# The first part of a scan-and-experts kernel in the order in which it is written, on every engine

## The chip, the cores and the metric

The kernel runs on one core of a Trainium2 chip. The metric is the time of one execution on the device, in microseconds (us); lower is better. The engines are TensorE (PE in the profile, its weight loads PEld), VectorE (DVE), ScalarE (ACT), GpSimd (POOL) and SyncE (SP), which here only issues transfers. A "q" behind an engine's name (SPq, POOLq) is its sequencer: branches, semaphores and the issuing of transfers.

## The reference

```python
def _attn_ref(x, f_logit, lower_bound):          # x, f_logit: (4, 5056, 256)
    sig = 1.0 / (1.0 + np.exp(-f_logit))
    f = lower_bound[None, None, :] + (1.0 - lower_bound[None, None, :]) * sig
    i = 1.0 - f
    for t in range(S):
        h = f[:, t] * h + i[:, t] * x[:, t]
        y[:, t] = h
...
def _moe_ref(x, w_gate, w_output_gate, w1, w2):  # 20224 tokens, 8 experts, 256 -> 1024 -> 256
    logits = x @ w_gate
    e_idx = np.argmax(logits, axis=1)
    ...                                          # gate_w: softmax probability of the chosen expert
    eom = 1.0 / (1.0 + np.exp(-(x @ w_output_gate)))
    for e in range(E):
        mask = e_idx == e
        h = np.maximum(x[mask] @ w1[e], 0.0)
        out[mask] = gate_w[mask, None] * eom[mask, e, None] * (h @ w2[e])
```

A gated running average over each sequence, and then every token through the one expert of eight that its gate picks.

## The kernel before

**Chunks.** The 20224 tokens are taken in 40 chunks of up to 512. `chunk(c)` is a generator: ACT and DVE scan the chunk, scale it and split it into two 16-bit halves; PE computes the gate (`pr`) and, from the one-hot choice `oh`, each token's rank in its expert (`pk`); DVE makes row numbers (`dst`) and factors (written into the rows' `meta`); SyncE transposes the halves into `rows`, and POOL scatters the rows by expert into a table in device memory (`scr`). Each bare `yield` ends a phase; `pump` runs one phase of every live chunk, with `together` mixing their small DVE instructions. Small tiles such as `dst` and `fac` come from pools with a fixed number of buffers (two where nothing else is said).

**Weights.** Ahead of the main part, 16 half-experts' weights are loaded, scaled and split into 16-bit parts: `prep_gram` (PE), `prep_norm`, `prep_scale` and `prep_lo` (DVE), `prep_hi` (ACT). The loop over `j` and its two half-steps `z` does this, and each half-step calls `step`, which pumps the chunks.

**First tiles.** In the same half-steps, 16 tiles of 128 tokens (two rounds over the experts) go through the experts that are ready. `early` gathers a tile (`gather`: a transposing transfer into `xq` and a small one into `mt`, both on SyncE's queue, after a load of the row number from a plan's table `pf_tab`), `first1` multiplies by w1 in two halves, `first_low` makes the low part of the result on DVE, `first2` multiplies by w2, `factors` makes the output factor `fac` from `mt`, `evacuate` scales (ACT), `put` scatters to the output (POOL).

**Main part.** `experts` runs 64 tiles of 256 tokens and 18 of 128 in the same manner, with the remaining chunks pumped between. Behind it stand 19 more tiles of 128 in two conditional blocks, run only if the plan counted more than 18 (`MORE`); with these inputs none runs.

**What sets the order.** A scheduler orders each engine's instructions by a simulated timeline, unless they are tied. `ordered` ties every instruction to the one written before it on its engine, except that ahead of `cut` (the end of the first part) it leaves DVE, ACT, PE and POOL loose:

```python
free = i < cut and ins.engine in loose
if ins.engine in prev and not free:
    tc.add_manual_dep(ins, prev[ins.engine], AFTER, reason="order")
```

So SyncE's queue is in the written order throughout, the others only from the main part on.

Of the kernel before, what the change touches and what calls it, by code (L numbers as in the profile page):

```python
# [50 lines left out]
def tile_scan_moe(  # L51
# [124 lines left out]

    gsq = cp.tile([P, KD * G], F32, name="gsq")
    gss = cp.tile([P, 1], BF16, name="gss")
# [31 lines left out]
    nc.gpsimd.iota(padt[:, CM + 2 : CM + 4].bitcast(I32), pattern=[[0, 1]], base=N, channel_multiplier=0)  # L210
    fresh.append(nc.sync.dma_start(out=scr[FREE : FREE + P, :], in_=padt))
    apart(fresh[0], "scr")
    row2 = [cp.tile([P, NB, RW], I16, name=f"rows{i}") for i in range(2)]
# [410 lines left out]
    def gather(t, slot, e=None):  # L624
        tab, j, nb, new = slot
        n = nb * P
        r = nc.sync.value_load(tab[j : j + 1, 0:1], min_val=0, max_val=FREE + P - n)
        xq = gp.tile([P, 2, KD, 256], I16, tag="xq", name="xq")
        mt = gp.tile([P, 2, 4], I16, tag="mt", name="mt", bufs=4)
        i1 = nc.sync.dma_start_transpose(  # L630
            out=xq.rearrange("p a k n -> p (a k) n")[:, :, 0:n], in_=scr[ds(r, n), 0 : 2 * D]
        )
        i2 = nc.sync.dma_start(out=mt[:, 0:nb, :], in_=scr[ds(r, n), CM : CM + 4].rearrange("(b p) d -> p b d", p=P))
        for ins in (i1, i2):
            for k in new:
                tc.add_manual_dep(raw(ins), raw(k).name, DATA, reason="rows scattered")
            apart(ins, "scr", new)
        return dict(xh=xq[:, 0].bitcast(F16), xl=xq[:, 1].bitcast(F16), mt=mt, nb=nb, tab=tab, j=j, id=t, ev=e)
# [5 lines left out]
    def factors(T):  # L644
        nb, ev = T["nb"], T["ev"]
        col = cinv[:, ev : ev + 1] if isinstance(ev, int) else cinv[:, ds(ev, 1)]
        fac = sp.tile([P, 2], F32, tag="fac", name="fac", bufs=4)
        yield SMALL
        nc.vector.tensor_scalar(  # L649
            fac[:, 0:nb].unsqueeze(2), T["mt"][:, 0:nb, 0:2].bitcast(F32), col, None, ALU.mult  # L650
        )
        T["fac"] = fac

# [68 lines left out]
    def first_low(T, h):  # L722
        ph, hh = T[f"h{h}"]
        hl = ep.tile([P, 4, P], F16, tag="el", name="el", bufs=3)
        yield BIG
        nc.vector.scalar_tensor_tensor(out=hl, in0=ph, scalar=0.0, in1=hh, op0=ALU.max, op1=ALU.subtract)
        T[f"h{h}"] = (hh, hl)
# [103 lines left out]
    def early(j):  # L831

        if not line or line[0]["half"] == 1 and len(line) == 1:
            for r in range(len(firsts)):
# [11 lines left out]
        for T, h in wait:  # L846
            tasks.append(first_low(T, h))
            if h == 0:
                tasks.append(factors(T))
# [27 lines left out]
    for n in range(min(EARLY[0], NCH) - 1, deep):  # L877
        prep_load(n)
    for j in range(-2, nh):
        tasks = []  # L880
# [29 lines left out]

    def ordered(start, cut):

        loose = [e.engine for e in (nc.vector, nc.scalar, nc.tensor, nc.gpsimd)]
        prev = {}
        for i, ins in enumerate(nc.cur_bb.bb.instructions[start:]):
            free = i < cut and ins.engine in loose
            if ins.engine in prev and not free:
                tc.add_manual_dep(ins, prev[ins.engine], AFTER, reason="order")
# [39 lines left out]
    between["on"] = True  # L958
    experts(0, total + cuts[0], len(cuts) - 1)
    beside()  # L960
    ordered(0, prog["cut"])

    if len(cuts) > 1:
        used = nc.values_load(prog["count"][0:1, 0:1], min_val=0, max_val=tail)  # L964
        for a, b in zip(cuts[:-1], cuts[1:]):
            with tc.If(used > a):
                experts(total + a, total + b, 0)
                ordered(0, 0)

# [37 lines left out]
```

## Time and profile before

| | us |
|---|---|
| median of three runs | 989.25 (988.75 to 989.73) |
| the profiled execution, its own time | 990.77 |
| its span, first to last instruction | 989.1 |
| busy in the span: PE, DVE, ACT, POOL | 907.7, 801.0, 519.7, 390.1 |
| the first matmul of the main part starts | 184.5 |
| the last output row is issued | 973.5 |
| mean granted PE clock | 0.988 |

Times in the rows are microseconds from the span's start. A row of a stretch gives its length, each engine's busy time with the count of instructions, the granted clock, the busy share of the 16 DMA engines and GB/s. A row of waits reads "who waited, for whom: us in all, times, longest". A row in order of time reads start, duration, engine, line, operation, tile written, tiles read, and in brackets the idle time ahead of it with what ended it. A row of one line's instructions gives shortest, median and longest duration in ns, and the first and last start.

### The profile page before, as it was taken

The page shows a single profiled execution, that of the slowest core. Times are in us where ns is not written, and L with a number is a line of the kernel's source. Part 1 is how long each engine was busy: PE and PEld are TensorE (multiplying, and loading weights), DVE is VectorE, ACT ScalarE, POOL GpSimd, SP SyncE. Part 2 cuts the span into 40 slices and gives each one's busy share as a digit, 9 for nine tenths or more (in the row PEclk, how much of TensorE's full clock was granted, in tenths as well). Part 3 has the DMA queues.
Part 4 walks back from the last instruction along what each step waited for, and adds up shares of the span by engine and source line. Part 5 has one row for each costly group of instructions (what it writes and reads, how often), then busy time and mean ns, then how long its engine had stood idle before and what let it go on. Part 6 is the DMA issues. An engine that isn't in the chain of part 4 may idle for free. (4 is left out here: it accounts for less than half of the span.)

```text
span 989.1 us, 30907 instructions
## 1 busy us (share of the span) xinstructions
PE 907.7 (92%) x9775; PEld 819.7 (83%) x9775; DVE 801.0 (81%) x2639; ACT 519.7 (53%) x1075; POOL 390.1 (39%) x378
## 2 busy tenths in 40 slices
PE   2258898899999999999999999999999999999993
PEld 2247887788888888888888888888888888899992
DVE  7989897888989988888898888888888886545550
ACT  6667675555555555555565555555555543333331
POOL 1432334434445454454545434455444443211111
PEclk9999999999999999999999999999999999999997
DMA  8899984855575657556576665655666544312120
GB/s 310 206 275 293 237 230 126 188 157 151 131 157 144 151 153 167 141 133 152 150 153 150 169 138 140 153 148 157 150 163 134 129 100 90 100 45 43 41 57 17
DMA packets 238558, 146.56 MB, mean 148 GB/s; under 512 B 202557, under 2 KB 204223, under 8 KB 238400
## 3 DMA queue, kind: packets, MB, share of 16 engines
q1 hardware_dynamic: 222752, 101.74, 44.9%
q0 software_dynamic: 15360, 42.74, 14.4%
q8 instruction: 95, 1.56, 0.7%
q14 instruction: 63, 0.52, 0.2%
q10 hardware_dynamic: 288, 0.02, 0.0%
HBM read 58.38 MB, written 44.49 MB: 104 GB/s over the span
## 5 line engine op out<-in xcount | busy, mean ns | idle before, releaser
L674 ACT ACTIVATE hh<-ph 128x512 f16<-128x512 f32 (+1 forms) x328 | 180.4, 550 | 307.8 <-PE ph L671 297.4
L669 PE MATMUL ph<-xq,w 128*128 128x256 f16 (+1 forms) x1312 | 330.4, 260 | 2.9 <-DMA xq<-scr 2.4
L671 PE MATMUL ph<-xq,w 128*128 128x256 f16 (+1 forms) x1312 | 331.1, 261 | 0.0
L670 PE MATMUL ph<-xq,w 128*128 128x256 f16 (+1 forms) x1312 | 330.9, 261 | 0.0
L750 POOL DMA_INDIRECT out_dram<-yo,mt x146 | 175.3, 1201 | 363.2 <-ACT yo L746 339.9
L704 PE MATMUL py<-w2s,hl 128*128 x1168 | 318.5, 273 | 0.0
L703 PE MATMUL py<-w2s,hh 128*128 x1168 | 318.4, 273 | 0.0
L702 PE MATMUL py<-w2s,hh 128*128 x1168 | 318.1, 272 | 0.0
L682 DVE SCALAR_TENSOR_TENSOR hl<-ph,hh 128x512 f16<-128x512 f32 (+1 forms) x328 | 204.9, 625 | 58.2 <-ACT hh L674 55.8
L433 POOL DMA_INDIRECT scr<-rows,dst x154 | 175.7, 1141 | 122.6 <-issue 109.3
L657 DVE COPY w<-w1s 128x2048 f16 x164 | 120.3, 734 | 35.1 <-PE ph L671 33.3
L669 PEld LDWEIGHTS <-w 128*128 128x128 f16 x1312 | 127.9, 98 | 14.3 <-DVE fac L649 2.7
L671 PEld LDWEIGHTS <-w 128*128 128x128 f16 x1312 | 128.0, 98 | 11.9
L670 PEld LDWEIGHTS <-w 128*128 128x128 f16 x1312 | 127.9, 97 | 9.7
L704 PEld LDWEIGHTS <-hl 128*128 128x128 f16 x1168 | 114.1, 98 | 13.8
L702 PEld LDWEIGHTS <-hh 128*128 128x128 f16 x1168 | 114.0, 98 | 11.4
L703 PEld LDWEIGHTS <-hh 128*128 128x128 f16 x1168 | 113.9, 98 | 10.6
L280 DVE TENSOR_TENSOR_SCAN xt<-ft,xt 128x512 f32<-128x512 f32 (+4 forms) x78 | 90.8, 1172 | 0.0
L746 ACT ACTIVATE yo<-py,fac 128x256 f32<-128x256 f32 x146 | 61.8, 468 | 26.7 <-PE py L704 26.1
L314 DVE SCALAR_TENSOR_TENSOR ft<-xt,sa,ft 128x512 f16<-128x512 f32 (+1 forms) x76 | 56.2, 744 | 20.1 <-ACT ft L265 18.3
L329 PEld LDWEIGHTS <-ft 128*128 128x128 f16 x600 | 51.7, 99 | 15.1 <-ACT ft L310 4.9
L310 ACT ACTIVATE ft<-xt,sa 128x512 f16<-128x512 f32 (+1 forms) x76 | 50.2, 707 | 23.3 <-DVE li L299 16.0
(171 smaller groups left out, 1298.7 us busy)
## 6 DMA issues: line engine op xcount, KB each, us to landing
ft<-in_fT_dram SPq DMA_DIRECT2D x37, 512.0 KB
xt<-in_xT_dram SPq DMA_DIRECT2D x37, 512.0 KB
w<-in_wT_dram SPq DMA_DIRECT2D x32, 512.0 KB
scr<-rows,dst POOLq DMA_INDIRECT x154
rows<-ft SPq DMA_TRANSPOSE x152
out_dram<-yo,mt POOLq DMA_INDIRECT x146
xq<-scr SPq DMA_TRANSPOSE x99
scr<-padt SPq DMA_DIRECT2D x9, 136.0 KB
```

What stands on the lines that cost most here:

```text
L280: nc.vector.tensor_tensor_scan(out=xt[:, k, a:z], data0=ft[:, k, a:z], data1=xt[:, k, a:z], initial=init, op0=ALU.mult, op1=ALU.add)
L433: ins = nc.gpsimd.indirect_dma_start(out=scr[:, :], out_offset=IOA(ap=dst[:, b : b + 1], axis=0), in_=rows[:, b, :], in_offset=None)
L657: nc.vector.tensor_copy(out=w, in_=w1f[:, ds(T["ev"] * (2 * WH) + h * 2 * QH, 2 * QH)])
L669: nc.tensor.matmul(out=o, lhsT=w[:, f, k, 0, :], rhs=T["xh"][:, k, 0:n], start=first, stop=False)
L670: nc.tensor.matmul(out=o, lhsT=w[:, f, k, 0, :], rhs=T["xl"][:, k, 0:n], start=False, stop=False)
L671: nc.tensor.matmul(out=o, lhsT=w[:, f, k, 1, :], rhs=T["xh"][:, k, 0:n], start=False, stop=last)
L674: nc.scalar.activation(hh[:, :, 0:n], ph[:, :, 0:n], AF.Relu)
L682: nc.vector.scalar_tensor_tensor(out=hl[:, :, 0:n], in0=ph[:, :, 0:n], scalar=0.0, in1=hh[:, :, 0:n], op0=ALU.max, op1=ALU.subtract)
L702: nc.tensor.matmul(out=o, lhsT=hh[:, i, c], rhs=wh, start=first, stop=False, skip_group_check=True)
L703: nc.tensor.matmul(out=o, lhsT=hh[:, i, c], rhs=wl, start=False, stop=False, skip_group_check=True)
L704: nc.tensor.matmul(out=o, lhsT=hl[:, i, c], rhs=wh, start=False, stop=last, skip_group_check=True)
L750: ins = nc.gpsimd.indirect_dma_start(out=out[:, :], out_offset=IOA(ap=T["mt"][:, b, 2:4].bitcast(I32), axis=0), in_=T["yo"][:, b, :], in_o ...
```

## The change

All engines are tied to the written order in the first part too. Five things go with it:

- A first tile is gathered whenever fewer than two wait in `line` (before: when none waits or the last has its first half behind it), and `mt` has 7 buffers instead of 4.
- `factors` of a first tile is called when its second half's low part has been made, and is tied behind that instruction (before: with the first half's); `fac` has 6 buffers instead of 4.
- The store of the pad rows to `scr` moves from the head of SyncE's queue to behind the first loads.
- The two conditionals in a row become one with the other nested in it; the tile behind the main part is no longer gathered ahead of the conditional.
- `gsq`, a set-up tile, shares the buffer of `lgp`.

```diff
-    gsq = cp.tile([P, KD * G], F32, name="gsq")
+    gsq = sp.tile([P, NB, 2 * G], F32, tag="lgp", name="gsq").rearrange("p b g -> p (b g)")[:, 0 : KD * G]
...
-    fresh.append(nc.sync.dma_start(out=scr[FREE : FREE + P, :], in_=padt))
-    apart(fresh[0], "scr")
...
-        mt = gp.tile([P, 2, 4], I16, tag="mt", name="mt", bufs=4)
+        mt = gp.tile([P, 2, 4], I16, tag="mt", name="mt", bufs=7)
...
-        fac = sp.tile([P, 2], F32, tag="fac", name="fac", bufs=4)
+        fac = sp.tile([P, 2], F32, tag="fac", name="fac", bufs=6)
...
+        if "low" in T:
+            tc.add_manual_dep(raw(ins), T["low"], AFTER, reason="the transfer has had its time")
...
-        nc.vector.scalar_tensor_tensor(out=hl, in0=ph, scalar=0.0, in1=hh, op0=ALU.max, op1=ALU.subtract)
+        ins = nc.vector.scalar_tensor_tensor(out=hl, in0=ph, scalar=0.0, in1=hh, op0=ALU.max, op1=ALU.subtract)
+        T["low"] = raw(ins).name
...
-        if not line or line[0]["half"] == 1 and len(line) == 1:
+        if len(line) < 2:
...
         for T, h in wait:
             tasks.append(first_low(T, h))
-            if h == 0:
+        for T, h in late:
+            if h == 1:
                 tasks.append(factors(T))
...
     for n in range(min(EARLY[0], NCH) - 1, deep):
         prep_load(n)
+    fresh.append(nc.sync.dma_start(out=scr[FREE : FREE + P, :], in_=padt))
+    apart(fresh[0], "scr")
...
-    def ordered(start, cut):
+    def ordered(start):
 
-        loose = [e.engine for e in (nc.vector, nc.scalar, nc.tensor, nc.gpsimd)]
         prev = {}
         for i, ins in enumerate(nc.cur_bb.bb.instructions[start:]):
-            free = i < cut and ins.engine in loose
-            if ins.engine in prev and not free:
+            if ins.engine in prev:
...
-    experts(0, total + cuts[0], len(cuts) - 1)
+    experts(0, total + cuts[0], 0)
     beside()
-    ordered(0, prog["cut"])
+    ordered(0)
+
+    def rest_of(i):
+        if i + 1 < len(cuts):
+            with tc.If(used > cuts[i]):
+                experts(total + cuts[i], total + cuts[i + 1], 0)
+                ordered(0)
+                rest_of(i + 1)
...
-        for a, b in zip(cuts[:-1], cuts[1:]):
-            with tc.If(used > a):
-                experts(total + a, total + b, 0)
-                ordered(0, 0)
+        rest_of(0)
```

Line numbers up to 209 are the same in both kernels; from there on those of the kernel after are 2 lower up to `gather`, and a few higher or lower behind it.

**SyncE's queue, at the very start.** `w2s` and `ft` receive the gate logits of chunks 0 and 1 (chunk 0 borrows the room of the last expert's weights), `xt` the values, `w` are weights. Before:

```order
L1003 UNCONDITIONAL_BRANCH
L211 DMA scr<-padt 128x544
L250 DMA w2s<-in_fT_dram 128x2x512
L251 DMA w2s<-in_xT_dram 128x2x512
L250 DMA ft<-in_fT_dram 128x2x512
```

Now:

```order
L248 DMA w2s<-in_fT_dram 128x2x512
L249 DMA w2s<-in_xT_dram 128x2x512
L248 DMA ft<-in_fT_dram 128x2x512
L249 DMA xt<-in_xT_dram 128x2x512
L564 DMA w<-in_wT_dram 128x1024 x2
L248 DMA ft<-in_fT_dram 128x2x512
L249 DMA xt<-in_xT_dram 128x2x512
L564 DMA w<-in_wT_dram 128x1024 x6
L881 DMA scr<-padt 128x544
```

The pad rows' store has moved behind fourteen loads.

**DVE, where chunk 2 gets its row numbers.** `dst_537` are the row numbers of chunk 2, `pos_530` its ranks, `w1s_126` here the halves of chunk 3 (borrowed room), `xt_466` chunk 4, `w_159` a weight. Before:

```order
L600 SCALAR_TENSOR_TENSOR cinv_94<-wi_300,wi_596 128x1
L455 TENSOR_TENSOR pf_m_1224<-boff_92,pf_done_565 128x8
L269 SCALAR_TENSOR_TENSOR xt_466<-ft_465,xt_466 128x512 x2
L314 SCALAR_TENSOR_TENSOR w1s_126<-w1s_126,sa_526 128x512
L142 TENSOR_SCALAR wv_675<-pb_653 128x1
L416 TENSOR_REDUCE dst_537<-pos_530 128x4
L314 SCALAR_TENSOR_TENSOR w1s_126<-w1s_126,sa_526 128x512
L619 SCALAR_TENSOR_TENSOR w2s_127<-w_159,ws_595,w2s_127 128x4x256
```

Now:

```order
L148 TENSOR_SCALAR xs_519<-xv_518 128x1
L150 TENSOR_SCALAR xi_520<-xs_519 128x1
L294 TENSOR_SCALAR sa_526<-na_101,xs_519 128x2
L297 TENSOR_TENSOR li_528<-xi_520,gi4_121 128x1
L401 TENSOR_TENSOR pos_530<-pk_507,cnt_471 128x32
L407 TENSOR_TENSOR cnt_534<-cnt_471,pk_507 128x8
L410 TENSOR_TENSOR pos_530<-pos_530,oh_487 128x32
L414 TENSOR_REDUCE dst_537<-pos_530 128x4
L417 TENSOR_REDUCE es_539<-ex_513 128x4
L419 TENSOR_SCALAR eg_515<-eg_515 128x4
L422 SCALAR_TENSOR_TENSOR fc_542<-es_539,eg_515 128x4
L426 RECIPROCAL fc_542<-fc_542 128x4
```

`dst_537` now stands ahead of all of chunk 4 and of the weights (two `L619` of the first expert stood ahead of it and now stand behind), and the small instructions of one chunk follow each other instead of those of three chunks and a plan.

**DVE, at the fourteenth first tile.** `fac_3050` is that tile's factor, `mt_2907` its row data; `el` are low parts of first tiles. Before:

```order
L345 TENSOR_TENSOR lgo_3042<-lgp_2978 128x64
L357 TENSOR_REDUCE mx_3052<-lgo_3042 128x4
L360 TENSOR_TENSOR dl_3055<-lgo_3042,mx_3052 128x32
L363 SCALAR_TENSOR_TENSOR key_3058<-dl_3055,rev_86 128x32
L142 TENSOR_SCALAR xv_3181<-pv_3107 128x1
L369 TENSOR_REDUCE km_3060<-key_3058 128x4
L649 TENSOR_SCALAR fac_3050<-mt_2907,cinv_94 128x1
L419 TENSOR_REDUCE es_3247<-ex_3176 128x4
```

Now, where its number is `fac_3183` and its row data `mt_2847`:

```order
L726 SCALAR_TENSOR_TENSOR el_3121<-ph_3066,eh_3091 128x512
L142 TENSOR_SCALAR xv_3179<-pv_3118 128x1
L647 TENSOR_SCALAR fac_3183<-mt_2847,cinv_94 128x1
L144 TENSOR_SCALAR xv_3179<-xv_3179 128x1
L726 SCALAR_TENSOR_TENSOR el_3182<-ph_3128,eh_3153 128x512
L146 TENSOR_SCALAR xv_3179<-xv_3179 128x1
L148 TENSOR_SCALAR xs_3180<-xv_3179 128x1
```

It now stands behind the tile's own second low part, two half-steps on; in SyncE's queue the same tile's gather has moved ahead of a pair of chunk transposes that it stood behind.

More of the change, by code (lines that the diff above doesn't have):

```diff
@@ L646, in factors @@
         col = cinv[:, ev : ev + 1] if isinstance(ev, int) else cinv[:, ds(ev, 1)]
-        fac = sp.tile([P, 2], F32, tag="fac", name="fac", bufs=4)
+        fac = sp.tile([P, 2], F32, tag="fac", name="fac", bufs=6)
         yield SMALL
-        nc.vector.tensor_scalar(
+        ins = nc.vector.tensor_scalar(
             fac[:, 0:nb].unsqueeze(2), T["mt"][:, 0:nb, 0:2].bitcast(F32), col, None, ALU.mult
         )
+        if "low" in T:
+            tc.add_manual_dep(raw(ins), T["low"], AFTER, reason="the transfer has had its time")
         T["fac"] = fac
```

## The prediction

> **What bounds the kernel now.** I read the page first, then busy time by stretches, then who waited for whom inside the first part, then the first microseconds and the last sixteen in order of time.
>
> The page, the span and its 40 slices (25 us each):
>
> ```profile
> span 989.1 us, 30907 instructions
> PE   2258898899999999999999999999999999999993
> DVE  7989897888989988888898888888888886545550
> DMA  8899984855575657556576665655666544312120
> ```
>
> From the eighth slice on TensorE (PE) is at 9 until the last; ahead of it no engine is alone at the top. The same by stretches; the first main tile's matmul starts at 184.5, so the first four rows are the first part:
>
> ```profile
> core 0: us, PE busy (x) PEld busy (x) DVE busy (x) ACT busy (x) POOL busy (x), PEclk, DMA share, GB/s
> 6.00:45.00 39.00, 11.82 (x140) 9.58 (x139) 32.85 (x131) 26.85 (x54) 8.78 (x8) 1.00 1.03 302
> 45.00:100.00 55.00, 33.71 (x453) 30.60 (x453) 49.24 (x164) 36.56 (x62) 16.80 (x18) 1.00 1.05 270
> 100.00:150.00 50.00, 46.52 (x674) 44.03 (x675) 43.80 (x142) 36.88 (x65) 16.93 (x17) 0.97 0.90 232
> 150.00:184.00 34.00, 29.72 (x388) 27.03 (x385) 25.81 (x95) 17.75 (x39) 14.81 (x14) 0.95 0.57 134
> 300.00:800.00 500.00, 500.00 (x4999) 448.47 (x4998) 443.35 (x1460) 275.58 (x581) 236.72 (x211) 1.00 0.62 149
> ```
>
> The main part is PE's alone (500 of 500 us), its order is not touched, and what VectorE (DVE) or the queues gain there is worth nothing. The change counts where the first main matmul starts, and behind the last. The first part has no single owner: loads until about 25 us, then DVE (49.2 of 55 us), then PE and DVE together (46.5 and 43.8 of 50). From 45 to 184 us DVE idles 139 - 118.9 = 20.1 us, and PE from 100 to 184 us 7.8. The waits there:
>
> ```profile
> PE ph L715 <- DMA xq<-scr: 12.8, 6, 3.7
> DVE fac L649 <- DMA mt<-scr: 8.5, 7, 3.8
> DVE el L726 <- ACT eh L719: 3.3, 4, 1.3
> ```
>
> DVE's largest single reason to stand still is the factor of a first tile (`fac`), whose row data (`mt`) has not landed: 8.5 us in seven waits.
>
> **The change, part by part.** Work is the same: 533 DVE instructions stand ahead of the main part's first copy in both orders, and all matmuls are kept.
>
> *1. The pad rows leave the head of SyncE's queue.* The first load waits today behind a store that needs `padt` from GpSimd (POOL):
>
> ```profile
> 0.83 0.38 ACTq L122 DMA_DIRECT2D lbt<-in_lbT_dram  x1
> 3.16 0.38 SPq L211 DMA_DIRECT2D scr<-padt  x1
> 3.60 0.42 SPq L250 DMA_DIRECT2D w2s<-in_fT_dram  x1
> 7.65 1.15 ACT L265 ACTIVATE w2s<-w2s 128x512 f32<-128x512 f32 x2 [4.65 <-DMA w2s<-in_fT_dram]
> 9.04 1.29 DVE L269 SCALAR_TENSOR_TENSOR w2s<-w2s 128x512 f32<-128x512 f32 x2 [3.66 <-DMA w2s<-in_xT_dram]
> ```
>
> ACT's queue issues at 0.83 what waits for nothing, so SyncE could start the loads there: 3.60 - 0.83 = 2.8 us earlier. ACT and DVE both wait for them (4.65 and 3.66 us), so the whole first part moves: -2.8, and between -2.8 and 0 if something else then holds it. The store, now behind 14 loads, is 0.4 us of SyncE's queue ahead of the first transposes, which wait for ACT anyway; the first gathers need it, and they wait for three chunks' scatters as well (the last of them is issued at 50.78, in a row below).
>
> *2. Factors later, first tiles gathered earlier.* `fac` moves behind the first matrix product's second half, two half-steps on, and `mt` has 7 buffers, so the 8.5 us of waits go: -8.5. Late next would be the matmuls on `xq`, which come a half-step sooner only where SyncE's order changes, in the last four first tiles; of PE's 12.8 us the last wait is of that kind:
>
> ```profile
> 164.74 0.23 PE L715 MATMUL ph<-xq,w1s 128*128 128x128 f16 x1 [3.26 <-DMA xq<-scr]
> ```
>
> Bounds: -8.5, and -4.2 if half of these waits only hid waits behind them.
>
> *3. Dependent neighbours on DVE.* This speaks against the change. Counted in the two orders, 29 of the 384 small DVE instructions ahead of the main part read what the instruction just before them wrote; in the written order 106 do (one chunk's chain runs through where the scheduler had mixed three). What that costs is seen in the trace, four mixed instructions and four in a chain:
>
> ```profile
> 165.71 0.18 DVE L419 TENSOR_REDUCE es<-ex 128x4 f32<-128x32 f32 x1
> 165.80 0.14 DVE L144 TENSOR_SCALAR xv<-xv 128x1 int32<-128x1 int32 x1
> 165.86 0.18 DVE L372 TENSOR_TENSOR oh<-key,km 128x32 bf16<-128x32 f32 x1
> 165.98 0.15 DVE L146 TENSOR_SCALAR xv<-xv 128x1 int32<-128x1 int32 x1
> ...
> 202.67 0.17 DVE L489 SCALAR_TENSOR_TENSOR pl_m<-pl_done,pl_n 128x8 f32<-128x8 f32 x1
> 202.87 0.17 DVE L492 TENSOR_SCALAR pl_mi<-pl_m 128x8 int32<-128x8 f32 x1
> 203.07 0.17 DVE L494 TENSOR_SCALAR pl_mi<-pl_mi 128x8 int32<-128x8 int32 x1
> 203.28 0.17 DVE L497 CAST pl_av<-pl_mi 128x8 f32<-128x8 int32 x1
> ```
>
> Mixed, they start 0.09 us apart ((165.98 - 165.71) / 3); in a chain 0.20 ((203.28 - 202.67) / 3). So 77 more chained ones cost 77 x 0.10 = +7.7 us of a DVE that has 20 us to spare in 139; between +4 (half of them fall where DVE would have waited) and +7.7. The Trainium skill's page "Perfetto Trace Analysis", section "Optimizing Scalar/DVE Operations", gives DVE about 60 ns of overhead for an instruction on SBUF and says that the profiled latency is about twice that, since the second half overlaps with the next instruction; by it the loss of the overlap is an estimated 77 x 0.06 = 4.6 us and the sum comes out 3.1 us lower. The rows above are at 0.10, and I go by them.
>
> *4. The third chunk's row numbers wait for the first chunk's scatter.* `dst` has two buffers. In the written order `dst` of chunk 2 stands early and DVE is held in it until the four scatters of chunk 0 have landed:
>
> ```profile
> 10.62 2.34 DVE L280 TENSOR_TENSOR_SCAN w2s<-w2s 128x512 f32<-128x512 f32 x2 [0.28 <-ACT w2s L274]
> 32.75 0.23 DVE L430 TENSOR_SCALAR w1s<-fc,xi 128x4 f32<-128x4 f32 x1
> 33.90 1.46 POOL L433 DMA_INDIRECT scr<-w1s,dst  x1 [30.50 <-DMA rows<-ft]
> 38.62 0.96 POOL L433 DMA_INDIRECT scr<-w1s,dst  x1 [0.30 <-issue]
> 45.23 0.17 DVE L416 TENSOR_REDUCE dst<-pos 128x4 int32<-128x32 f32 x1
> 50.78 0.96 POOL L433 DMA_INDIRECT scr<-rows,dst  x1 [0.30 <-issue]
> 54.04 0.14 POOL L398 IOTA rows<- 128x4 int32 x1 [2.13 <-DMA scr<-rows,dst]
> ```
>
> Today 12.5 us lie between chunk 0's factors (32.75) and that `dst` (45.23). The scatters take 39.58 - 32.75 = 6.8 us from there and 2.3 to land (54.04 - 51.74): 9.1, so nothing waits. In the written order only two multiplies and two scans of chunk 3 (1.29 + 2.34, and 0.3 for a norm), 17 mixed instructions (17 x 0.09 = 1.5) and ten chained ones (2.0) stand between: 7.4. DVE stands 9.1 - 7.4 = +1.7 us; between 0 and +3 (one scatter took 2.0 us where most take 0.96). All of DVE's later work waits with it.
>
> *5. Every other wait in the strict order.* Nothing may overtake now: a matmul on a late `xq` holds gate, norm and rank matmuls behind it on PE, and a late ACT copy holds DVE. Against that each step of the written order asks for what the step before it made. The trace can't show it; I keep the other 11.6 us of DVE's idle time (20.1 - 8.5) as they are: 0, between -6 (half of it filled) and +8 (two thirds of PE's 12.8 us passed on to DVE).
>
> *6. One conditional instead of two.* No tile of the conditional blocks runs. After the last output row POOL goes through both:
>
> ```profile
> 973.55 0.98 POOL L750 DMA_INDIRECT out_dram<-yo,mt  x1 [2.08 <-ACTq L966]
> L966 PEldq COMPARE_BRANCH  x2: 3852/4162/4472, 972.9 to 977.1; - x2
> L966 POOLq COMPARE_BRANCH  x2: 45/45/45, 973.9 to 976.5; - x2
> L966 POOLq INC_SWDGE_SEM  x2: 2322/2328/2335, 974.2 to 977.0; - x2
> L1003 POOLq DRAIN  x3: 40/107/8885, 979.4 to 988.8; - x3
> ```
>
> From 973.9 two rounds of a branch and a semaphore catch-up (2.33 us each) lead to a drain at 979.4 that lasts 8.9 us and sets the end. Nested, one round goes: 976.5 - 973.9 = -2.6 if the drain keeps its length; 0 if it ends with something else, -5.2 if it also gets shorter by as much. PE loses one branch of about 4 us too, but is through its second at 977.1 + 4.5 = 981.6, ahead of the drain's end. The gather of one tile that no block used goes from SyncE's queue; PE covers it.
>
> The sum: -2.8 - 8.5 + 7.7 + 1.7 + 0 - 2.6 = **-4.5 us**. A second way, in case PE and not DVE sets 100 to 184 us: of DVE's `mt` waits these fall ahead of that,
>
> ```profile
> DVE fac L649 <- DMA mt<-scr: 1.4, 3, 0.9
> ```
>
> and of the 77 chained neighbours 36. Then the start gives -2.8, the wait in 4 +1.7, 36 x 0.10 = +3.6, the `mt` waits -1.4, PE's last `xq` wait -3.3, the end -2.6: -4.8. The profiled execution took 990.77 us (989.1 of span and 1.7 around it) and goes to 986.3; the median of the three runs, 989.25, is 1.5 under it and goes to **984.7 us**, my forecast.
>
> **The rivals.**
>
> A. *The strict order fills DVE's gaps.* DVE's 20.1 us go by half beyond the `mt` waits (term 5 at -6), or the chained ones cost half. For it: every input is made a step ahead. Against: PE has 7.8 us to give from 100 us on. 984.7 - 6 = 978.7; the floor with everything good is about 976.
>
> B. *No change.* The first part's terms cancel (start and factors against chains and strictness) and the drain ends where it ends: 989.25. For it: terms 2 and 3 are nearly equal and both rest on DVE being the bound.
>
> C. *Slower: PE is held by one late gather and everything behind it.* Today PE's six `xq` waits (12.8 us) let ready work through on other engines. If gate and norm matmuls queue behind them, DVE's norms and ranks wait too. At two thirds passed on, +8.5, the time is 993; it decides from +4.5 on, a bit over a third. For it: PE has 46.5 of 50 us busy from 100 to 150, so nothing there is caught up. Against: the late `xq` at 164.7 is gathered ahead of the transposes that it waits behind today.
>
> **How the numbers follow.** A measurement of this kernel tells 0.2%, 2 us, from no change (the runs span 1 us). Forecast, 981 to 987.3: 0.40. A, under 981: 0.22. B, 987.3 to 991.2: 0.17. C, over 991.2: 0.21. So faster 0.62, same 0.17, slower 0.21. The range reaches from A's floor to C's 993: 976 to 993 leaves out less than 2 in 10; the likeliest case alone is 981 to 987.3.
>
> **What would show it.** Right: first load issued near 0.8 us; no DVE wait on `mt`; DVE's small instructions in the first part busier by some 7 us; a DVE wait of 1 to 3 us before chunk 2's `dst` on the scatter; the first main matmul near 182 us instead of 184.5; one catch-up at the end and the drain starting 2.6 us sooner after the last put. Wrong: the first main matmul over 187 us with PE waits on `xq`, or ACT and DVE waits that repeat every half-step; or a drain that ends 14.7 us after the last put again.

## The result, and the profile after

| | before | after |
|---|---|---|
| median of six runs each, on one chip | 990.55 us (988.75 to 994.41) | 1000.5 us (998.81 to 1004.41) |
| ratio, 95% interval | | 1.0107 [1.0083, 1.0131] |
| span of the profiled execution | 989.1 | 1002.6 |
| the first main matmul starts | 184.5 | 199.5 |
| from there to the end of the last `py` matmul | 788.2 | 787.2 |
| from there to the end of the span | 16.4 | 15.9 |

The change makes the kernel 1.1% slower, about 10 us; the forecast was 984.7 and the range ended at 993. The whole loss lies ahead of the first main matmul, which comes 15.0 us later in the profiled executions. The main part and the end are each a little shorter. The profiled execution of the kernel after is the slowest of its six (1004.41 us, 3.9 over the median), so some 4 of its 15.0 us are that execution's own.

The page of the kernel after, its slices as before (25 us each), with the granted clock:

```profile
span 1002.6 us, 30868 instructions
PE   1266978799999999999999999999999999999993
DVE  7897967789888888888989888888988886545551
PEclk9997988999999999999999999999999999999997
DMA  9797984576666566656576755565667544322120
```

PE falls from 8 to 6 in the fourth slice and from 9 to 7 in the sixth, DVE from 9 to 7 and from 9 to 6 in the same two, and the clock row dips there and in the seventh (before, it was 9 throughout but for the last slice). The same stretches as before show where it builds up:

```profile
core 0: us, PE busy (x) PEld busy (x) DVE busy (x) ACT busy (x) POOL busy (x), PEclk, DMA share, GB/s
6.00:45.00 39.00, 9.78 (x132) 8.11 (x132) 31.86 (x122) 24.96 (x53) 10.15 (x12) 1.00 0.93 283
45.00:100.00 55.00, 33.36 (x409) 29.42 (x407) 48.42 (x164) 35.30 (x58) 19.08 (x16) 0.88 0.91 246
100.00:150.00 50.00, 41.84 (x605) 39.73 (x603) 40.80 (x129) 29.02 (x50) 16.25 (x15) 0.93 0.95 226
150.00:184.00 34.00, 30.16 (x393) 27.99 (x391) 25.33 (x76) 18.83 (x41) 12.26 (x12) 0.90 0.52 133
300.00:800.00 500.00, 500.00 (x4990) 448.25 (x4988) 442.03 (x1472) 274.74 (x579) 234.60 (x207) 1.00 0.62 150
```

From 45 to 150 us PE has done 1014 matmuls instead of 1127, and from 100 to 150 both PE (41.8 us for 46.5) and DVE (40.8 for 43.8) are busy less. So neither is the bound there: they wait for each other. For whom, in the waits of the first 200 us:

```profile
PE pv L289 <- ACT ft L285: 21.3, 12, 5.2
PE ph L715 <- DMA xq<-scr: 14.5, 3, 6.2
DVE jk L583 <- PE pg L576: 7.8, 3, 7.0
DVE el L726 <- ACT eh L719: 6.9, 8, 1.6
DVE jk L583 <- PE pv L289: 5.0, 1, 5.0
DVE dst L414 <- DMA scr<-w1s,dst: 3.3, 1, 3.3
```

The waits on `mt` are gone, as forecast. In their place DVE waits for the gram matmuls of the weights (`pg`, read by the norm `jk`): 12.8 us in four waits, two of which are 5.0 and 7.0. In order of time the first of the two is seen on all engines:

```profile
87.68 1.71 POOL L431 DMA_INDIRECT scr<-rows,dst  x1 [0.30 <-issue]
91.00 1.25 SPq L628 DMA_TRANSPOSE xq<-scr  x1
93.77 0.27 PE L715 MATMUL ph<-xq,w1s 128*128 128x128 f16 x1 [6.19 <-DMA xq<-scr]
96.28 0.42 PE L736 MATMUL py<-w2s,eh 128*128 128x256 f16 x1
98.74 1.08 PE L576 MATMUL pg<-w 128*128 128x128 bf16 x16
99.86 0.29 DVE L583 SCALAR_TENSOR_TENSOR jk<-pg,ident 128x128 f16<-128x128 f32 x1 [4.98 <-PE pv L289]
```

The gather needs rows whose last scatter is issued at 87.68; it goes out at 91.00, and PE stands 6.19 us ahead of the first product of that first tile. Then come, in the written order, that tile's products (2.5 us), the second products of the tile before (96.28, 2.5 us more), and only at 98.74 the sixteen gram matmuls, which waited for nothing but their turn (with the order of `gram_first`, below, they run at 88.32 without a wait). DVE, which needs them next, stands 4.98 us.

The 5 us of held work are so long because PE has half its clock there: the granted clock is 0.50 from 94 to 98 us, and the first products start 0.107 us apart, where those at 85 us start 0.055 apart. At full clock the 24 first and 12 second products would take some 2.6 us (24 x 0.055 + 12 x 0.109, the second from 139.7 on). By the clock column of the stretches, half clock adds up to some 27 us between 45 and 184 us, and to some 7 in the kernel before. The second place is the same:

```profile
119.04 2.54 SPq L305 DMA_TRANSPOSE rows<-ft  x2
126.05 0.39 SPq L248 DMA_DIRECT2D ft<-in_fT_dram  x1
128.71 1.23 SPq L628 DMA_TRANSPOSE xq<-scr  x1
136.59 0.29 PE L715 MATMUL ph<-xq,w1s 128*128 128x128 f16 x1 [5.98 <-DMA xq<-scr]
141.78 0.29 DVE L583 SCALAR_TENSOR_TENSOR jk<-pg,ident 128x128 f16<-128x128 f32 x1 [7.04 <-PE pg L576]
```

Here the gather is issued at 128.71 behind a chunk's load that waited for two transposes, and PE can start at 136.59, 7.9 us later (PE waits 5.98); two megabytes of loads were issued just ahead of it. DVE stands 7.04, and here too the granted clock is 0.50 (136.5 to 139.4 us).

### The profile page after: what moved, and what is told of

It is laid out like the page before. It is cut to its first block, busy times and chain, and to the rows that moved or that the text cites. A ratio compares the mean times of both kernels' runs of the same rounds, so it can differ in the third digit from the quotient of the medians.

```text
span 1002.6 us, 30868 instructions
## 1 busy us (share of the span) xinstructions
PE 912.1 (91%) x9775; PEld 822.8 (82%) x9775; DVE 803.9 (80%) x2639; ACT 518.7 (52%) x1075; POOL 397.1 (40%) x378
## 4 chain that ended last, share of the span: by engine, by line
PE 72%; issue 11%; DVE 9%; POOL 2%; DMA 2%; ACT 2%; POOLq 0%; DVEq 0%; SPq 0%; ACTq 0%
PE ph L669 11%; PE py L702 11%; PE ph L670 11%; PE ph L671 11%; PE py L704 11%; PE py L703 11%; POOL out_dram L751 2%; DVE xt L278 2%; DVE w1s L617 1%; DMA xq<-scr 1%; PE pr L327 1%; PE ph L715 1%; PE ph L716 1%; PE ph L717 1%; PE py L736 1%
## 5 line engine op out<-in xcount | busy, mean ns | idle before, releaser
L751 POOL DMA_INDIRECT out_dram<-yo,mt x146 | 172.5, 1182 | 362.3 <-ACT yo L747 341.1
L682 DVE SCALAR_TENSOR_TENSOR hl<-ph,hh 128x512 f16<-128x512 f32 (+1 forms) x328 | 204.7, 624 | 60.1 <-ACT hh L674 58.2
L431 POOL DMA_INDIRECT scr<-rows,dst x154 | 186.1, 1208 | 134.5 <-issue 116.0
L657 DVE COPY w<-w1s 128x2048 f16 x164 | 117.4, 716 | 35.2 <-PE ph L671 33.5
L702 PEld LDWEIGHTS <-hh 128*128 128x128 f16 x1168 | 113.9, 98 | 11.4
L703 PEld LDWEIGHTS <-hh 128*128 128x128 f16 x1168 | 113.9, 98 | 10.6
L715 PE MATMUL ph<-xq,w1s 128*128 128x128 f16 x256 | 49.0, 231 | 14.5 <-DMA xq<-scr 14.5
```

Of the source, the lines that this page charges most:

```text
L431: ins = nc.gpsimd.indirect_dma_start(out=scr[:, :], out_offset=IOA(ap=dst[:, b : b + 1], axis=0), in_=rows[:, b, :], in_offset=None)
L657: nc.vector.tensor_copy(out=w, in_=w1f[:, ds(T["ev"] * (2 * WH) + h * 2 * QH, 2 * QH)])
L682: nc.vector.scalar_tensor_tensor(out=hl[:, :, 0:n], in0=ph[:, :, 0:n], scalar=0.0, in1=hh[:, :, 0:n], op0=ALU.max, op1=ALU.subtract)
L702: nc.tensor.matmul(out=o, lhsT=hh[:, i, c], rhs=wh, start=first, stop=False, skip_group_check=True)
L703: nc.tensor.matmul(out=o, lhsT=hh[:, i, c], rhs=wl, start=False, stop=False, skip_group_check=True)
L751: ins = nc.gpsimd.indirect_dma_start(out=out[:, :], out_offset=IOA(ap=T["mt"][:, b, 2:4].bitcast(I32), axis=0), in_=T["yo"][:, b, :], in_o ...
```

## The experiments

The eighteen runs below ran on two chips on which the kernel before took 1006 to 1013 us instead of 990.6 (`before_again`, `after_again`, `gram_first` and `old_gather` on one, all others on the second). So each ratio is to the kernel before, run beside it, and traces are compared among themselves. On those chips PE also stands in the main part, in gaps for which the profile shows no releaser: 3 to 11 us in all by kernel. They go with the length of the main part, from 793.7 us (`dve_loose`, 3.4 us of gaps) to 807.6 (`gf_dst3`, 11.4), although the order of the main part is the written one in all of them. That is up to 1.4% between two executions, and no matter of the first part; so the first main matmul is the better measure here, and it is one execution each.

**Which engine's order?** In the kernel after, one engine (or all four) is left to the scheduler again ahead of the main part:

```diff
+            free = i < cut and ins.engine in loose     # loose: PE / DVE / ACT / all four
-            if ins.engine in prev:
+            if ins.engine in prev and not free:
```

> The kernel after, with PE alone left to the scheduler ahead of the main part; DVE, ACT, POOL and SyncE stay in the written order. Theory 1 (PE is held: in the first 200 us of the kernel after PE waits 21.3 + 6.0 + 3.3 us for ACT's Square ahead of a norm matmul (pv) and 14.5 + 6.1 us for a gathered tile (xq), and every gram, gate, rank and first-tile matmul is queued behind): the first main matmul comes back from 199.5 to 188 or sooner, the time from 1000.5 to 989 or less. Theory 2 (DVE's written order, more dependent neighbours and nothing to fill a gap with): the first main matmul stays over 196, the time over 997. Theory 3 (ACT's written order: the Square stands behind weight copies that wait for DVE's scale, 11.4 + 10.1 us): as theory 2. Theory 4 (not the order but the gathers a tile ahead and the later factors): as theory 2.

> The kernel after, with DVE alone left to the scheduler ahead of the main part. Theory 1 (PE is held by late inputs): little comes back, the first main matmul stays over 195 and the time over 996, unless DVE's freer order brings the inputs sooner. Theory 2 (DVE's written order costs): the first main matmul at 188 or sooner, the time 989 or less; the DVE work of 45 to 150 us busier than the 89.2 of 105 us that it has in the kernel after. Theories 3 and 4: over 196, over 997.

> The kernel after, with ACT alone left to the scheduler ahead of the main part. Theory 3 (ACT's written order: a Square or another copy stands behind a weight copy that waits for DVE's scale): the waits of PE's pv for the Square go from 30 us to under 12, the first main matmul to 188 or sooner, the time to 989 or less. Theories 1 and 2: the first main matmul stays over 195, the time over 996. Theory 4: over 197.

> The kernel after with DVE, ACT, PE and POOL all left to the scheduler ahead of the main part, as before; the other edits stay (pad store behind the loads, gathers a tile ahead, factors two half-steps later, nested conditional). Theories 1, 2 and 3 (the written order costs): the prediction's other terms are left: first load at 0.8 instead of 3.6 (-2.8), the waits on mt gone (-1 to -8), the end -0.5 as the kernel after shows: first main matmul at 173 to 182, the time 979 to 987, faster than before. Theory 4 (gathers and factors cost): first main matmul over 190, time over 994.

| kernel | ratio to before [95%] | first main matmul |
|---|---|---|
| PE loose | 1.0084 [1.0054, 1.0114] | 198.8 |
| DVE loose | 1.0043 [1.0012, 1.0073] | 200.0 |
| ACT loose | 1.0196 [1.0145, 1.0248] | 206.2 |
| all loose | 1.0016 [0.9976, 1.0055] | 194.1 |

With all loose the loss is gone within the interval: the order carries most of it, and the other edits together bring no gain clear of noise, where the prediction gave them 13.9 us. No single engine gives the first part back. DVE loose has the lowest ratio of the three, but its first main matmul stands at 200.0; its main part is the shortest of all (793.7 us). A loose ACT makes it worse, which no theory expected: its trace has a PE wait of 7.0 us on `xq` at 98 and a DVE wait of 5.7 on `jk` at 104 (why they grew stays open), and a long main part besides (805.7 us). Theory 1 fell in its simple form (PE loose). Its waits show why, of the kernel with PE loose:

```profile
PE ph L715 <- DMA xq<-scr: 17.8, 7, 4.0
DVE jk L583 <- PE ph L717: 7.5, 2, 6.3
```

The scheduler, which does not know how late `xq` is, puts first tiles ahead of gram matmuls as well: PE still takes them in some fixed order, waits 17.8 us, and DVE stands 6.3 us in `jk` once more. Loose is not the same as free. All loose shows the pair as well (PE waits 4.1 us on `xq` at 74, DVE 5.6 on `jk` at 80) without a loss against the kernel before; whether that is what its other gains went into is not shown.

**The gram matmuls ahead of the first tile, and the old gathering.** `gram_first` moves PE's order alone, `old_gather` SyncE's alone (in the traces the orders of the other engines are those of the kernel after):

```diff
-            rest()                      # first tiles: evacuate, put, first1, first2
             tasks = []
             if j + 2 < nh:
                 ...                     # prep_gram and prep_norm, or prep_sum
+            rest()
```

```diff
-        if len(line) < 2:
+        if not line or line[0]["half"] == 1 and len(line) == 1:
```

> The kernel before once more, for its profile on the chip that the next three run on (the four with one or more engines left loose ran on a chip on which the kernel before took 1007.5 us instead of 990.6, so their times in the trace cannot be held against the first two traces): ratio 1.000. If all_loose is in fact no different from it, its first main matmul stands within 3 us of the 194.1 that all_loose shows, on such a chip.

> The kernel after once more, on the same chip as before_again: ratio 1.008 to 1.013 as in the first comparison (1.0107), first main matmul 10 to 16 us later than in before_again. If the loss depends on the chip, the ratio lies outside; then dve_loose's 1.0043 and pe_loose's 1.0084 say nothing yet of the engines. Two waits of DVE of 4 to 8 us on gram matmuls (jk on pg) right behind PE waits of about 6 us on xq are to be seen again if theory C holds.

> The kernel after with one thing written earlier: the gram matmuls and the norm sum of the weights stand ahead of the first tiles' matmuls in each half-step instead of behind them; PE's order alone changes. Theory C (PE is held by a late xq and the gram matmuls queue behind it, so that DVE stands 5.0 and 7.0 us on jk): the jk waits over 2 us go, the first main matmul comes 8 to 12 us sooner than in after_again, ratio to before 0.998 to 1.003. Rival (the loss is spread over many short waits of the strict order, and the two long ones only hide others): under 4 us come back, ratio 1.006 or more.

> The kernel after with the old rule for gathering a first tile (when none waits or the last has its first half behind it); SyncE's queue alone changes, the four other engines keep their order. Theory S (the gathers moved ahead stand in SyncE's queue in front of chunk transposes and blocks follow: a wait of 4.3 us for the transposes ahead of a chunk's load, then the load ahead of the next gather, whose 7.8 us landing holds PE 6.0): the second long PE wait on xq goes, 4 to 8 us come back, ratio 1.003 to 1.006. Theory C without S: the gathers come later still, PE waits on xq grow, ratio 1.010 to 1.020. If SyncE's order does not matter: as after_again within 2 us.

| kernel | ratio to before [95%] | first main matmul |
|---|---|---|
| before again | 0.9997 [0.9976, 1.0018] | 193.2 |
| after again | 1.0106 [1.0060, 1.0151] | 201.7 |
| gram first | 1.0000 [0.9973, 1.0028] | 193.4 |
| old gathering | 1.0168 [1.0131, 1.0205] | 208.5 |

The loss is there again on this chip, smaller at the first main matmul (8.4 us for 15.0), and with one block of PE's order moved it is gone: 8.3 us. The main parts of after again and gram first are of one length (800.0 and 799.9 us). The clock is not what makes the difference: between 45 and 184 us PE has half clock for 17 us in after again and 20 in before again. Waits up to the main part, first of after again, then of gram first:

```profile
PE ph L715 <- DMA xq<-scr: 10.6, 5, 6.2
DVE jk L583 <- PE pv L289: 4.6, 1, 4.6
DVE jk L583 <- PE pg L576: 4.1, 5, 1.5
```

```profile
ACT eh L719 <- PE ph L717: 20.9, 13, 3.1
PE pb L590 <- DVE jk L583: 11.2, 6, 3.7
DVE el L726 <- ACT eh L719: 10.6, 8, 3.4
PE ph L715 <- DMA xq<-scr: 4.3, 2, 4.1
DVE dst L414 <- DMA scr<-w1s,dst: 2.6, 1, 2.6
```

`jk` is no longer among DVE's waits (8.7 us before), and PE's own wait on `xq` falls from 10.6 to 4.3, because the gram matmuls now use the time in which the tile lands. Theory C is shown for this kernel: it is a late `xq` with ready work behind it. PE's longest wait in sum, for ACT's Square ahead of a norm matmul (`pv` on `ft`), mostly stays (19.0 us after again, 14.2 gram first), so the loss is not that. Of the two long `jk` waits that were expected, after again has only the first (4.6 us behind an `xq` wait of 6.2); the second, of 7.0 us in the first comparison, is not seen again, which fits the smaller loss.

Theory S fell: with the old gathering PE's waits on `xq` are 15.9 us in seven and `jk` waits of 5.1, 4.6 and 6.2 us follow, the ratio rises by 0.006. Gathering a tile ahead is a gain in the written order; without it the change would have cost 1.7%.

**The prediction's terms, one by one, on gram first.** DVE loose as above; the pad store back at the head; a third tile gathered ahead (`len(line) < 3`); three buffers for `dst`:

```diff
-        dst = small("dst", None, I32)
+        dst = sp.tile([P, NB], I32, tag="dst", name="dst", bufs=3)
```

> gram_first with DVE left to the scheduler ahead of the main part. Theory K (dependent neighbours on DVE cost what term 3 said: small DVE instructions ahead of the main part are busy 49.0 us in gram_first and 42.1 in before_again): small ones back to 42 to 44, DVE's idle time stays near 31.3, the first main matmul 4 to 7 us sooner than in gram_first, ratio 0.993 to 0.997. Rival (the scheduler's order of DVE stands out of step with the written order of ACT and PE, and what is saved in busy time comes back as waits): busy falls all the same, idle rises by as much, ratio 0.999 to 1.004.

> gram_first with the pad store back at the head of SyncE's queue. If term 1 of the prediction holds (the whole first part moves with the first load): first load at 3.6 instead of 0.8, first main matmul 2.8 us later, ratio 1.002 to 1.004. If the early start is lost again at the wait for chunk 0's scatter and the loads that follow: the first scans 2.8 us later, that wait shorter, first main matmul within 1 us, ratio as gram_first (1.000).

> gram_first with a first tile gathered whenever fewer than three wait (instead of two). Theory C goes on: the PE waits on xq that are left (4.1 us at 93, 0.2 elsewhere) shrink unless their rows are not scattered yet: up to 3 us sooner, ratio 0.997 to 1.000. Rival S (gathers further ahead make SyncE wait for scatters in front of chunk transposes and loads): 3 to 8 us later, ratio 1.003 to 1.008.

> gram_first with three buffers for the row numbers instead of two; every engine's order stays. If term 4 of the prediction is on the path (DVE stands 2.6 us at 40.5 until chunk 0's scatters have landed): the wait goes, the first main matmul 1.5 to 2.6 us sooner, ratio 0.997 to 0.9985. If the next input is late anyway: the wait moves to the gate's or the scan's input, no change.

| kernel | ratio to before [95%] | first main matmul |
|---|---|---|
| DVE loose | 1.0029 [1.0003, 1.0056] | 193.3 |
| pad store at the head | 1.0070 [1.0042, 1.0098] | 196.8 |
| three gathered ahead | 1.0020 [0.9997, 1.0043] | 192.4 |
| `dst` with three buffers | 1.0063 [1.0030, 1.0096] | 191.2 |

DVE loose: the stretch of 6 to 192 us, of gram first and then of this kernel:

```profile
6.00:192.00 186.00, 126.63 (x1651) 113.43 (x1650) 158.78 (x534) 116.36 (x216) 64.75 (x60) 0.95 0.83 225
```

```profile
6.00:192.00 186.00, 126.26 (x1652) 112.56 (x1651) 153.79 (x539) 115.62 (x214) 64.55 (x59) 0.95 0.82 225
```

DVE is busy 5.0 us less for the same work and the first main matmul stands where it stood (193.3 for 193.4): the saved time comes back as idle time. The rival's reading holds: the chained neighbours cost busy time on DVE and next to nothing at the end. (Gram first's second execution, on the chip of this kernel, has its first main matmul at 195.7, so up to 2.3 of the 5.0 us may arrive there; the ratio shows none of it.)

With the pad store at the head the first load is at 3.40 and the first main matmul at 196.8, where the three others of the table and gram first stand at 191.2 to 195.7: 3.4 and 1.2 us behind gram first's two executions, about what term 1 has. The ratio is 0.004 to 0.007 above theirs but for the three `dst` buffers, more than the first part explains. A third tile ahead changes nothing: the wait on `xq` at 94 us stays 4.15 us, since the gather that it waits for keeps its place in SyncE's queue; only the gathers from 101 us on move. Three `dst` buffers take DVE's wait at chunk 2 away and shorten the first part by 2.2 to 4.4 us, yet the time is 0.6% up: from the first main matmul to the last `py` this kernel takes 807.6 us where gram first takes 799.9 (and 803.3 in its second run), with PE gaps without a releaser of 11.4 us for 5.6 (and 7.7). The instruction order is the same on every engine, so this is not the first part. It needs no third buffer either: three gathered ahead has 804.8 us with 9.3 of gaps. The cause of the gaps stays open.

**PE alone, and the pad store alone, in the kernel before.** `pe_tied` takes `nc.tensor` out of `loose` in the kernel before, `pe_tied_gf` also writes the gram matmuls first, `b_pad` only moves the pad store. These are not one change each: what is loose is ordered anew by the scheduler. Of DVE's 533 instructions ahead of the main part about half in `b_pad`, and two thirds in `pe_tied`, stand in another order than in the kernel before (267 and 353 fall outside the longest matches of the traces), and some of ACT's and PE's too.

> The kernel before with PE alone tied to the written order ahead of the main part; DVE, ACT and POOL stay loose, and none of the other edits is made. Theory C (PE is held by a late xq and the gram matmuls queue behind): PE waits of 3 us and more on xq with DVE waits on jk right behind, first main matmul 8 to 17 us later than before's 184.5 to 193.2 (depending on the chip), ratio 1.008 to 1.017. Rival (the loss needs the written order of DVE and ACT as well): ratio 0.998 to 1.004.

> pe_tied with the gram matmuls and the norm sum written ahead of the first tiles' matmuls. Theory C: the DVE waits on jk go, ratio 0.998 to 1.004 and at least 0.006 under pe_tied. Rival (it is PE's place for other matmuls, gate or norm, that costs): within 0.004 of pe_tied.

> The kernel before with only the pad store moved behind the first loads. Term 1 on its own: first load at 0.8, first main matmul 1 to 3 us sooner, ratio 0.997 to 0.999. If the start is lost again at a later wait: 1.000.

> gram_first once more, beside pe_tied_gf and b_pad. If its level is that of the kernel before: 0.998 to 1.002. If the variants' 1.002 to 1.007 is its level on their chip: 1.003 or more.

| kernel | ratio to before [95%] | first main matmul |
|---|---|---|
| PE tied | 1.0129 [1.0096, 1.0162] | 204.7 |
| PE tied, gram first | 1.0089 [1.0061, 1.0117] | 203.9 |
| pad store moved | 1.0030 [1.0003, 1.0058] | 198.5 |
| gram first, second time | 1.0015 [0.9991, 1.0038] | 195.7 |

PE's written order, with what the scheduler then makes of the others, costs as much as the whole change. That it costs it by theory C is not shown: the DVE waits on `jk` of 2 us and more (5.1 at 122 us, 2.0 at 146) do not stand behind PE's waits on `xq` (62, 94, 105 and 205 us). Writing the gram matmuls first gives back only 0.004 here, with overlapping intervals, as the rival has it: the waits on `xq` go from 14.0 to 4.9 us, and PE now waits 9.3 us for the weights of a gram matmul:

```profile
PE pg L578 <- DMA w<-in_wT_dram: 9.3, 4, 5.5
PE ph L715 <- DMA xq<-scr: 4.9, 2, 2.8
DVE fac L649 <- DMA mt<-scr: 4.7, 4, 2.6
```

In this mixture one late input is exchanged for another. So theory C explains the kernel after, where nothing but PE's order was moved; it is not a rule that gram first is right.

The pad store moved in the kernel before gains nothing (the interval lies above 1), though the first load is at 0.82. What the start gained is lost at the gathers, and more:

```profile
DVE fac L647 <- DMA mt<-scr: 12.8, 6, 3.5
PE ph L713 <- DMA xq<-scr: 12.4, 4, 4.4
```

against 2.9 and 11.3 us in before again. With the new order of DVE, and the clock at 0.5 of full speed from 30 to 64 us in this execution, neither the 198.5 nor these waits can be put down to the store alone. Gram first stands at 1.0015 on this chip: level with the kernel before within 0.4% on both.

**First products last.** If a late `xq` should hold nothing, the second products can go ahead of the first ones too. `gf_swap` exchanges the two in `rest` of gram first (POOL's queue differs by one output scatter, which comes three places later); `gf_swap_dst3` adds the third `dst` buffer.

```diff
+            for T, h in late:
+                first2(T, h)
+                ...
             if go:
                 ...
                 first1(T, h)
-            for T, h in late:
-                first2(T, h)
-                ...
```

> gram_first with the second matrix products (first2) written ahead of the first ones (first1) in each half-step, so that a late xq holds nothing that is ready; PE's order alone changes. Theory C carried to its end: PE's wait on xq at 93 goes from 4.1 to under 2 us, the first main matmul 1 to 3 us sooner than gram_first's 193.4 to 195.7, ratio 0.996 to 1.000. Rival: the first products, now up to 2.7 us later in each half-step, make ACT's copies (eh) and DVE's low parts (el) late; DVE's waits on eh rise over the 10.6 us of gram_first, ratio 1.001 to 1.006.

> gf_swap with three buffers for the row numbers. Term 4 (2.6 to 4.3 us of DVE's wait on chunk 0's scatter): 1 to 3 us less than gf_swap. If gf_dst3's 1.0063 was an effect of that edit and not of its runs: 4 us and more slower than gf_swap, with PE gaps without a releaser in the main part of over 10 us in all (gf_dst3: 12.5; gram_first: 6.2 and 8.2).

The ratios are 1.0072 [1.0044, 1.0099] and 1.0113 [1.0072, 1.0155], the first main matmuls stand at 203.3 and 201.6. The rival is right. Of `gf_swap`, up to the main part:

```profile
DVE el L726 <- ACT eh L719: 22.2, 11, 6.8
PE ph L715 <- DMA xq<-scr: 3.4, 1, 3.4
```

PE waits less for `xq` (3.4 for 4.3 us) and DVE twice as long for the first products' copies (22.2 for 10.6). The three buffers again shorten the first part (by 1.7 us) and again lengthen the rest: 804.9 us from the first main matmul to the last `py`, for 798.2.

No version ran faster than the kernel before by more than the noise.

## Why the prediction was wrong

By its own steps, in the profiled executions of the first comparison. DVE up to its first copy of the main part is the ledger: 183.8 us before, of which 154.7 busy and 29.1 idle; 198.75 after, of which 160.9 and 37.8 (union of its instructions in the trace; "small" are those under 0.45 us, counted where no other covers them). On the chip of before again it reads 154.9 busy and 37.6 idle before, 161.6 and 39.3 after, 161.0 and 31.4 with gram first.

1. *Pad store, -2.8.* The first load is issued at 0.82, as forecast. In the written order it is worth 1.2 to 3.4 us of the first part (`gf_pad_head`); in the kernel before nothing arrives (`b_pad`), with another order on DVE. What does not hold everywhere is "the whole first part moves".
2. *Factors later, -8.5.* No DVE wait on `mt` is left: right as a wait. With the four engines loose these edits show no gain (`all_loose`), but that does not tell how many of the 8.5 us hid others: on the other chip the kernel before has only 2.9 us of these waits to begin with (before again). In the written order the earlier gathers are worth something after all: 0.006 against the old rule (`old_gather`). The step also had it that SyncE's order changes only in the last four first tiles; in the trace the fifth gather already stands earlier (at 97.3 us, ahead of a chunk's two loads), and so do the seventh and the eighth (each ahead of a pair of chunk transposes).
3. *Dependent neighbours, +7.7.* Small instructions ahead of the main part are busy 49.4 us instead of 42.3: +7.1. The price was right. (The estimate of 4.6 us from the Trainium skill's page "Perfetto Trace Analysis", section "Optimizing Scalar/DVE Operations", is too low beside it.) That it is paid at the end was wrong, or mostly: `gf_dve_loose` takes 5.0 us of it away, and the time is no shorter.
4. *`dst` behind chunk 0's scatter, +1.7.* DVE waits 3.3 us at 41 us (2.2 to 4.3 in the other kernels); `gf_dst3` has its first main matmul 2.2 to 4.4 us sooner than gram first. Right in place, under its size by half.
5. *Every other wait, 0 (-6 to +8).* This is the step that failed. Terms 1, 2 and 4 would have left 29.1 - 2.8 - 8.5 + 1.7 = 19.5 us of idle time on DVE; it has 37.8. So the strict order's other waits cost 18.3 us instead of 0 (1.6 of them are term 4's), and 12.0 are the two `jk` waits. On the other chip the idle time was to fall by 9.6 us and rose by 1.7: 11.3 us more than the sum had, 8.7 of them `jk`; `gram_first`, which takes the `jk` waits away, brings 7.9 us of it back. The bound of +8 was two thirds of PE's `xq` waits of before. It missed two things: those waits themselves grow when nothing can go ahead of them (6.2 and 6.0 where the longest was 3.7), and what stands behind pays more than the wait, since the late tile's own products and the second products of the tile before, 5 us together, run first, and run at half clock, which no term had. The sign that the prediction named for being wrong is what came: the first main matmul over 187 us with PE waits on `xq`. Its second way of adding up (-4.8) was no check on this, since it left the same waits out.
6. *One conditional, -2.6.* From the last put to the drain 5.35 us instead of 5.83: -0.5. The rows of the end, after:

```profile
L967 PEldq COMPARE_BRANCH  x1: 3705/3705/3705, 986.8 to 986.8; - x1
L967 POOLq COMPARE_BRANCH  x1: 45/45/45, 987.8 to 987.8; - x1
L967 POOLq INC_SWDGE_SEM  x1: 2346/2346/2346, 990.5 to 990.5; - x1
L1009 POOLq DRAIN  x3: 40/107/8885, 992.8 to 1002.3; - x3
```

POOL's branch is over at 987.9, but its catch-up starts only at 990.5. What it waits for is the last put: the trace has the last update of that transfer's semaphore at 990.35, 2.87 us after the put's start, and the wait on this semaphore stands right ahead of the catch-up. In all fifteen traces with one conditional the catch-up starts 0.11 us behind that landing, which comes 2.58 to 3.11 us after the put. With two conditionals the first catch-up (0.61 to 2.94 us after the put) ran while the rows were landing (2.82), and the second followed. So the step failed in taking the second round for the one on the path: one round less saves only what lay behind the landing. (PE's branch, 3.7 us long, ends near the catch-up's start here, but later than it in others: 3.15 us after the put in after again, where the catch-up starts at 2.94.)

Rival C named the mechanism, gate and norm matmuls queued behind a late gather, with the place (DVE's norms) and a chance of 0.21, and priced it at +8.5; the sum with the other terms then gave 993, the end of the range. The median rose by 10 us and ended at 1000.5: C's own cost was larger than its price, and of the gains set against it (terms 1, 2 and 6, 13.9 us) the runs show only parts.

## What to carry to other kernels

- On an engine that takes its queue in order, price a late input by what stands behind it: the wait, plus the work of the held step itself, for whoever needs the next ready instruction. Put ready work that others wait for (here the weights' gram matmuls) between the request of an input and its first use.
- A busy saving or an earlier start counts only if the next input is there: the `mt` waits went as forecast, and DVE's 5.0 us of overlap came back, and neither made the kernel faster; DVE's idle time took up the second (31.4 us in gram first, 37.2 with DVE loose).
- Between two chains that share an engine there is an order that serves both, and moving one item further can cost more than it gives: gram matmuls first gave 8.3 us, second products first took 8 to 10 back.
- An experiment on an order that a scheduler makes is seldom one change: moving one store in the kernel before put about half of DVE's instructions in another order. Compare the orders in the traces before putting a difference down to the edit.

## What was not expected of the hardware

- The end is paced by the landing of the last scatter, then POOL's catch-up (2.32 to 2.35 us) and its drain (8.885 us in every run here). PE's branch over a block that is not taken takes 3.7 to 4.5 us, where those of DVE, ACT and POOL take 0.05 to 0.07; it is not what the catch-up waits for.
- In the first part PE's granted clock falls to 0.50 in stretches of 3.4, 6.8 or 10.2 us (one of 34 in `b_pad`). In the kernel after two of them, 88.4 to 98.6 and 132.7 to 139.5 us, cover the long waits on `xq` and the products behind them, so the work behind a late input was slow as well as late.
- The same program is 1.6 to 2.2% slower on the chips of the experiments. In part this is the main part (797.1 us for 788.2 in the kernel before, with PE gaps of 5.3 us in all where the first comparison shows none); these gaps, 0.1 to 0.9 us each, often lie about 22 to 23 us apart or a multiple of it (after again: 234.4, 257.5, 280.2, 303.4). The Trainium skill's page "Runtime: NRT & Kernel Launch", section "Instruction fetch mechanics", says that each engine's instructions come in blocks of 16 KiB through a DMA queue of its own, mostly hidden. The traces show such a queue, with a packet of 16384 bytes every 10 us or so, in the first comparison as well; gaps at every second packet would fit that, but no run here tested it.
